# A quarter of the first expert weight by the hardware DMA queue, and a new written order for attention

## The chip, the cores and the metric

The kernel runs on one core of one Trainium2 chip. The core has a matrix engine (PE, whose weight loads are listed as PEld), a vector engine (DVE), a scalar engine (ACT), GpSimd (POOL), a sync engine (SP), and 16 DMA engines that all its queues share. The metric is the device time of one execution in microseconds (us), lower is better; of several runs the median is taken.

## What is computed

The first half is attention over 4 batches, 8 heads, 768 positions and head dimension 64. The integer input `is_retrieval` splits the heads: retrieval heads see all earlier keys, the others see the first 4 keys and the last 64.

```python
scores = scale * np.matmul(q, k.transpose(0, 1, 3, 2))
scores = np.where(mask, scores, -1000000000.0)
a = np.exp(scores - max); a = a / (sum(a) + 1e-09)
attn = np.matmul(a, v)
```

The second half is a soft mixture of 8 experts with 4 slots each over the 3072 rows x (512 wide) that attention gives:

```python
logits = x @ phi                                  # 3072 x 32
d = softmax(logits, over rows);  slot_input = d.T @ x
h = relu(slot_input[e] @ w1[e]);  slot_out[e] = h @ w2[e]      # 8 experts
out = softmax(logits, over slots) @ slot_out
```

w1 is 8 x 512 x 1024 and w2 is 8 x 1024 x 512, in float32. Inputs are 52.5 MB, the output is 6.3 MB.

## The kernel before

**Loads.** q, k and v of one batch (`load_raw`, L270) and one 512 x 1024 weight of an expert (`load_w`, L283) are each one DMA that POOL issues (L252) on the software queue; this queue turns float32 into bf16 on the way. There are 12 raw loads of 1.57 MB and 16 weight loads of 2.10 MB, as float32. They go into 11 slots of 8 KB per partition, and the last five weights (11 to 15, `late_mem`, L744) into memory that attention has left: weight 14 into `pt_mem` after PV.14.5, weight 15 into `qk_mem` after the last score matmul. Before the change nothing is loaded by SP; ACT issues two small loads (L363, L364).

**Attention.** Heads are worked in 16 pairs p = 4b + n, where b is the batch. Raw q, k, v are transposed on PE (`T` operations, L476, four per tensor and batch) and evicted from PSUM by `E` operations through the helper `copy` (L243), by DVE or by ACT. Score blocks (`QK`, L501) go into two PSUM buffers. ACT takes the exponential (`EX`, L572, five per pair, each 128 x 1024) into `pt_mem`, DVE multiplies the mask in (`MK`, L518), PE multiplies by v (`PV`, L632), DVE normalises (`NM`, L644 and L646), PE transposes the result (`XT`, L658) and a copy `XE` stores it. v needs a second transpose (`V2`, L535), a copy `VB` and a masked copy `VF` (L551). Ek1.3 is the eviction of the fourth quarter of batch 1's k, VB.7 the copy of pair 7's v, and so on.

**The tail.** After pair 15 come the logits (`LG`), their exponential (`EL`), the slot sums (`DS`, `SA`, `SI`, `SIE`), the first expert product `H` (L808) with its relu `HR`, transposes `TH`, evictions `HE`, and then the eight `W2.e` steps in order, e = 0 to 7 (L846), of eight matmuls each. W2.7 needs weight 15. Its result is scaled by ACT (`SO`, L854), multiplied out in 25 pieces (`OM`, L873; `OE`, L880 and L882) and stored by SP in 8 DMAs (L892).

**Order.** A list scheduler, class `Plan`, fixes the order of all of this when the kernel is built. Every operation has a duration per engine, dependencies, buffers to take and free, a due key (`T` = 6.2 us per pair), and for some a `lead`, the earliest start. `run` (L62) picks, among what could start within 0.12 us of the earliest, the smallest key. Where an operation names two engines (`copy_engs = {"DVE": 0.56, "ACT": 0.81}`), the scheduler picks one. `LAT` holds what it adds between an operation's end and its use on another engine. Each engine then executes its instructions strictly in the order so written.

**Fillers.** `emit_zb` (L377) starts PE with 13 matmuls on zeros. After the schedule is made, a second loop (L919 to L961) puts more zero matmuls (L965) where the plan leaves PE idle: ahead of an operation that starts by 22 us, about one for each 0.215 us of the planned gap; and in the tail, up to the start of the W2 steps.

```python
gap, at = max(o.start + shift - free, 0.0), free
unit = 0.427 if slow else 0.215
n = int((gap - 0.1) / unit + 0.5) if gap > 0.2 else 0
```

Here `o.start` is the planned time and `free` the planned end of what stands before on PE; the plan gives the 13 first matmuls 0.30 us each.

Of the kernel before, what the change touches and what calls it, by code (L numbers as in the profile page):

```python
# [10 lines left out]
F32 = mybir.dt.float32  # L11
# [4 lines left out]
ACT = mybir.ActivationFunctionType  # L16
PSUM = bass.MemoryType.PSUM
KB = 512


class Buf:


# [9 lines left out]
class Plan:  # L33


    LAT = {"PE": 0.20, "ACT": 0.06, "DVE": 0.08, "POOL": 0.15, "DMA": 0.40, "SP": 0.05}
    OVERLAP = {"ACT": 0.10, "DVE": 0.085}
    SWITCH, BONUS, ACTPEN = 0.13, 4.0, 0.4

# [4 lines left out]

    def op(self, name, engs, key, deps=(), acq=(), rel=(), emit=None, lead=0.0, need=(), n=0):
        o = Op()
        o.name, o.engs, o.key, o.emit = name, engs, key, emit
        o.deps = [d for d in deps if d is not None]
        o.acq, o.rel, o.end, o.eng, o.succ, o.lead = list(acq), list(rel), None, None, [], lead
        o.kind = ("r" if name[0] == "Q" else "c" if name[0] == "T" and name[1] in "qkv" else  # L50
                  "g" if name[:2] in ("DS", "H.", "W2") else "f")
        o.need = [b for b in list(need) + o.rel if b not in o.acq]
        for b in o.rel:
            b.rels += 1
            b.left += 1
        o.ndep, o.n = len(o.deps), n
        for d in o.deps:
            d.succ.append(o)
        self.ops.append(o)
        return o  # L60
# [88 lines left out]
def kernel(  # L149
# [13 lines left out]
    nc = tc.nc  # L163
    P = 128
    B, H, S, D = q.shape
# [13 lines left out]
    pt_mem = sb.tile([P, 20 * KB], BF16, name="pt")  # L179
# [10 lines left out]
    ident = sb.tile([P, P], BF16, name="ident")  # L190
# [12 lines left out]
    flag = sb.tile([P, 2, H], BF16, name="flag")  # L203
# [46 lines left out]
    def dma(name, key, nbytes, ndesc, buf, dst, src, deps=()):  # L250
        iss = pl.op("issue " + name, {"POOL": 0.62}, key, deps=deps, acq=[buf] if buf else [], lead=1.3,
                    emit=lambda o: nc.gpsimd.dma_start(dst(), src))  # L252
        issues.append(iss)
        return pl.op("land " + name, {"DMA": dma_us(nbytes, ndesc)}, key, deps=[iss], lead=2.8)

    def dma_us(nbytes, ndesc):
        return ndesc / 16 * 0.0225 + nbytes / 16 / 27170.0
# [12 lines left out]
    def load_raw(x, b, key):  # L270
        raws[x, b] = buf = Buf("S8")
        lands[x, b] = dma(f"{x}{b}", key, 96 * 2 * 8192, 192, buf, lambda: raw_view(buf, 0, 96), raw_src(x, b, 0, 4))
# [6 lines left out]
    def w_view(i):  # L279
        m = late_mem[i]() if i in late_mem else slots[wbuf[i].slot][:, :]  # L280
        return m.rearrange("p (a f) -> p a f", a=4 if i < NE else 8)

    def load_w(i, key, deps=()):  # L283
        if i < NE:
            src = moe_w1[i].rearrange("(di do) f -> di do f", do=4)
        else:
            src = moe_w2[i - NE].rearrange("(fi fo) d -> fi fo d", fo=8)
        wland[i] = dma(f"w{i}", key, 2 << 20, 128, None if i in late_mem else wbuf[i],
                       lambda: w_view(i), src, deps=deps)
# [72 lines left out]
    def sp_front(o):  # L362
        nc.scalar.dma_start(ri, ri_src)  # L363
        nc.scalar.dma_start(phf, moe_phi.rearrange("(di do) s -> di do s", do=4))  # L364

    load_raw("q", 0, -99)
    o_iss = pl.op("issue small", {"ACT": 1.0}, -98, emit=sp_front, lead=0.7)
    o_sp = pl.op("land small", {"SP": 0.1}, -98, deps=[o_iss], lead=3.0)
# [10 lines left out]
            nc.tensor.matmul(pvb[:, 1, :], zero[:, 0:128], zero, start=True, stop=True, skip_group_check=True)  # L379

    o_zb = pl.op("ZB", {"PE": 0.30 * NZ}, -100, n=NZ, emit=emit_zb, lead=1.2)
    o_id = pl.op("ident", {"DVE": 0.5}, -80, deps=[o_tab], emit=head_const)
    o_kp = pl.op("key_pos", {"DVE": 2.3}, -79, deps=[o_id, o_tq], emit=key_pos)
    o_fl = pl.op("flag row", {"DVE": 0.35}, -79.5, deps=[o_sp], emit=flag_row)
    o_fl = pl.op("FB", {"PE": 0.1}, -78, n=1, deps=[o_fl, o_zb], acq=[flb], emit=flag_bc)
    o_fl = pl.op("flags", {"DVE": 1.0}, -78, deps=[o_fl, o_kp], rel=[flb], emit=flags)

# [2 lines left out]
            nc.gpsimd.memset(b_[:, :, :, :, 64:66], 1.0)  # L390

    o_one = pl.op("ones", {"POOL": 0.4}, -40, deps=[issues[2]], emit=pone)
    o_fm = pl.op("far mask", {"ACT": 1.6}, -39, deps=[o_fl], emit=far_mask)
    o_hm = {}
    for n in range(4):
        o_hm[n] = [pl.op(f"hm{n}.{i}", {"DVE": 0.55}, -28.5 if n == 0 else T * n - 2.0, deps=[o_fl],
                         emit=lambda o, h=n + 4 * i: head_mask(h)) for i in range(2)]
    o_st = pl.op("slot tables", {"DVE": 1.2}, T * 8, deps=[o_id], emit=slot_tables)

    phb = xT.rearrange("p a c -> p (a c)")[:, 2048:2176].rearrange("p (o s) -> p o s", o=4)  # L400
    ph2 = xT.rearrange("p a c -> p (a c)")[0:NS, 2304:2816]
# [396 lines left out]
    for e4 in range(2):  # L798
        hse[e4] = []
        for c in range(2):  # L800
            hp = Buf("SC" if c == 0 else "TR")
            h_buf = hp if e4 == c == 0 else h_buf
            bank = (lambda hp=hp: scb[hp.slot][:, 0, :]) if c == 0 else (lambda hp=hp: trb[hp.slot])

            def emit_h(o, e4=e4, c=c, bank=bank):
                for do in range(4):
                    for g in range(4):
                        nc.tensor.matmul(bank()[32 * g:32 * (g + 1), :], siT[:, do, :],  # L808
                                         w_view(4 * e4 + g)[:, do, c * 512:(c + 1) * 512],
                                         start=(do == 0), stop=(do == 3), tile_position=(0, 32 * g))  # L810

            a = pl.op(f"H.{e4}.{c}", {"PE": 0.86}, kt + 1, n=16, deps=[o_sie] + [wland[4 * e4 + g] for g in range(4)],
                      acq=[hp], emit=emit_h)

            def emit_hr(o, e4=e4, c=c, bank=bank):
                d, s_ = hs_t[e4][:, c, :], bank()
                if o.eng == "ACT":
                    nc.scalar.activation(d, s_, ACT.Relu, scale=emask[:, e4:e4 + 1])
                else:
                    nc.vector.tensor_scalar(d, s_, emask[:, e4:e4 + 1], 0.0, op0=ALU.mult, op1=ALU.max)  # L820

            hse[e4].append(pl.op(f"HR.{e4}.{c}", {"ACT": 0.7, "DVE": 0.76}, kt + 1, deps=[a, o_st],
                                 rel=[hp], emit=emit_hr))
        th = Buf("SC")

        def emit_th(o, e4=e4, th=th):
            t = scb[th.slot][:, 0, :].bitcast(BF16)
            hv = hs_t[e4].rearrange("p c f -> p (c f)").rearrange("p (fi fo) -> p fo fi", fo=8)
            for fo in range(8):
                nc.tensor.transpose(t[:, 128 * fo:128 * (fo + 1)], hv[:, fo, :], ident)  # L830

        a = pl.op(f"TH.{e4}", {"PE": 0.5}, kt + 2, n=8, deps=hse[e4], acq=[th], emit=emit_th)

        def emit_he(o, e4=e4, th=th):
            copy(o, hT_t[e4].rearrange("p f c -> p (f c)"), scb[th.slot][:, 0, :].bitcast(BF16))

        hte[e4] = pl.op(f"HE.{e4}", {"DVE": 0.7, "ACT": 1.02}, kt + 2, deps=[a], rel=[th], emit=emit_he)
# [81 lines left out]
    for o in order:  # L919
        if o.eng != "PE":  # L920
            continue
        if o is o_zb:
            hist += [(o.start + 0.30 * (x + 1), 512) for x in range(NZ)]
            free = o.end
            continue
        gap, at = max(o.start + shift - free, 0.0), free
        tail = at >= last_pv - 0.01 and o.start <= w_last.start + 0.01
        front = o.start <= 22.0
        if front:
            start = max(o.start + shift, free)  # L930
            slow = start < 4.2
            unit = 0.427 if slow else 0.215
            n = int((gap - 0.1) / unit + 0.5) if gap > 0.2 else 0
            for _ in range(n):
                hist.append((free + unit, 512))
                free += unit
            took = (o.end - o.start) * (1.7 if slow else 1.0)
            while o.start > 4.5:
                e = max(free, o.start + shift) + took
                got = sum(a for t, a in hist if t > e - FW) + area(o.name)  # L940
                if got >= FA or n >= 6:
                    break
                n += 1
                free += unit
                hist.append((free, 512))
            free = max(free, o.start + shift) + took
            hist.append((free, area(o.name)))
            if n:
                if at < first_pv:
                    before[o.name] = (n, 0, pvb[:, 1, :], 0)  # L950
            continue
        free = o.end
        gap = o.start - at
        if gap < 0.25 or not tail or (at >= by_name["W2.0"].end - 0.01 and o is not w_last):
            continue
        if o is w_last:
            continue
        bank, c0 = (scb[h_buf.slot] if o.start <= h_first + 0.01 else pvb)[:, 1, :], 0
        us, w = gap - 0.12, 512 - c0
        n = max(0, int(us / (w / 2400)))  # L960
        before[o.name] = (n, max(0, int((us - n * w / 2400) / 0.0534)), bank, c0)  # L961

# [45 lines left out]
```

## Time and profile before

| | |
|---|---|
| median of 3 runs | 153.15 us (153.1 to 153.8) |
| the profiled execution | 152.3 us |
| its span, first to last instruction | 150.4 us |
| busy: PE, DVE, ACT, POOL | 126.7, 112.1, 109.7, 17.9 us |
| software queue (loads) | 26.22 MB written as bf16, 85.4% of the 16 engines' span |
| hardware queue (stores) | 6.29 MB, 10.3% |
| mean granted TensorE clock | 0.973 |

All durations below are of the one profiled execution. A busy PE is not a PE at its peak, and the share of a DMA engine can pass 1 where its packets overlap. The engines' busy times are means over stages that have different limits, so a stage has to be looked at by itself. A line number is that of the kernel before.

### The profile page before, as it was taken

The page shows a single profiled execution, that of the slowest core. Times are in us where ns is not written, and L with a number is a line of the kernel's source. Part 1 is how long each engine was busy: PE and PEld are TensorE (multiplying, and loading weights), DVE is VectorE, ACT ScalarE, POOL GpSimd, SP SyncE. Part 2 cuts the span into 40 slices and gives each one's busy share as a digit, 9 for nine tenths or more (in the row PEclk, how much of TensorE's full clock was granted, in tenths as well). Part 3 has the DMA queues.
Part 4 walks back from the last instruction along what each step waited for, and adds up shares of the span by engine and source line. Part 5 has one row for each costly group of instructions (what it writes and reads, how often), then busy time and mean ns, then how long its engine had stood idle before and what let it go on. Part 6 is the DMA issues. An engine that isn't in the chain of part 4 may idle for free.

```text
span 150.4 us, 5213 instructions
## 1 busy us (share of the span) xinstructions
PE 126.7 (84%) x2299; PEld 81.6 (54%) x2304; DVE 112.1 (75%) x232; ACT 109.7 (73%) x132; POOL 17.9 (12%) x37
## 2 busy tenths in 40 slices
PE   6999999988899999698999899999779999797000
PEld 2355566757667676565757667666457446332000
DVE  3879579989689979967998978979866495099000
ACT  3053899997998999689999999999993243299000
POOL 6911110101110001210000112110011000000000
PEclk9999999999999999999999999999999999999955
DMA  3999999999999999999999999999999997069993
GB/s 40 190 215 220 220 206 211 216 221 216 211 211 217 217 220 218 218 205 215 212 219 228 211 200 211 218 218 213 213 216 213 222 218 163 13 229 438 425 420 161
DMA packets 6120, 32.90 MB, mean 219 GB/s; under 512 B 594, under 2 KB 722, under 8 KB 3410
## 3 DMA queue, kind: packets, MB, share of 16 engines
q0 software_dynamic: 4800, 26.22, 85.4%
q1 hardware_dynamic: 1152, 6.29, 10.3%
q8 instruction: 18, 0.29, 0.7%
q10 hardware_dynamic: 146, 0.07, 0.2%
q14 instruction: 4, 0.03, 0.1%
HBM read 52.49 MB, written 6.29 MB: 391 GB/s over the span
## 4 chain that ended last, share of the span: by engine, by line
PE 31%; DMA 20%; issue 15%; ACT 13%; DVE 12%; POOL 2%; DVEq 0%; POOLq 0%; ACTq 0%
DMA qk<-in_moe_w_dram 11%; ACT pt L572 9%; DMA slot<-in_v_dram 9%; PE tr L476 8%; PE pv L632 8%; PE sc L501 8%; DVE slot L882 3%; DVE pt L518 2%; DVE xv L646 2%; PE tr L658 2%; DVE vf L551 1%; ACT xv L245 1%; ACT vx L596 1%; DVE vx L247 1%; PE tr L673 1%
## 5 line engine op out<-in xcount | busy, mean ns | idle before, releaser
L572 ACT ACTIVATE pt<-sc 128x1024 bf16<-128x1024 f32 x80 | 77.0, 1054 | 4.3 <-PE sc L501 4.1
L501 PE MATMUL sc<-qk 64*128 64x512 bf16 (+3 forms) x256 | 31.0, 307 | 4.4 <-ACT pt L572 2.7
L518 DVE TENSOR_TENSOR pt<-pt,msk 128x1024 bf16<-128x1024 bf16 (+1 forms) x48 | 30.6, 640 | 1.8 <-ACT pt L572 1.6
L632 PE MATMUL pv<-vx,pt 128*128 128x65 bf16 x352 | 27.2, 193 | 0.3 <-DVE pt L518 0.2
L632 PEld LDWEIGHTS <-pt 128*128 128x128 bf16 x640 | 23.6, 97 | 6.9 <-issue 4.1
L476 PE MATMUL tr<-ident,slot 96*64 96x96 bf16 x704 | 20.8, 208 | 2.2 <-issue 1.8
L476 PEld LDWEIGHTS <-slot 96*64 96x64 bf16 x768 | 18.3, 110 | 8.0 <-issue 5.9
L632 PE MATMUL pv<-vf,pt 128*128 128x65 bf16 x288 | 21.4, 194 | 0.0
L501 PEld LDWEIGHTS <-qk 64*128 64x128 bf16 x256 | 11.0, 93 | 12.6 <-issue 6.3
L646 DVE TENSOR_TENSOR xv<-pv,rs 128x768 bf16<-128x768 f32 x16 | 15.3, 958 | 0.6
L247 DVE COPY qk<-tr 128x768 bf16<-128x768 bf16 x22 | 11.8, 551 | 1.5 <-PE tr L476 1.3
L252 POOL DMA_DIRECT2D slot<-in_moe_w_dram x11 | 6.0, 550 | 41.1 <-PE tr L476 31.7
L247 DVE COPY xT<-tr 128x768 bf16<-128x768 bf16 x15 | 8.3, 553 | 1.1 <-PE tr L658 1.1
L658 PE MATMUL tr<-ident,xv 128*128 128x128 bf16 x96 | 8.0, 220 | 1.1 <-DVE xv L646 0.9
L247 DVE COPY xv<-tr 128x768 bf16<-128x768 bf16 x10 | 5.5, 555 | 3.7 <-PE tr L476 3.5
L245 ACT COPY qk<-tr 128x768 bf16<-128x768 bf16 x6 | 4.8, 816 | 4.3 <-PE tr L476 4.2
L658 PEld LDWEIGHTS <-xv 128*128 128x128 bf16 x96 | 5.8, 97 | 3.9 <-issue 1.8
L535 PE MATMUL tr<-ident,xv 128*128 128x128 bf16 x96 | 7.8, 220 | 0.1
L965 PE MATMUL pv<-zero 128*128 128x512 bf16 (+1 forms) x31 | 7.4, 365 | 0.5 <-issue 0.5
L551 DVE TENSOR_TENSOR vf<-vx,fm 128x528 bf16<-128x528 bf16 x16 | 6.7, 429 | 1.2 <-ACT vx L245 1.0
L644 DVE RECIPROCAL rs<-pv 128x12 f32<-128x12 f32 x16 | 3.7, 230 | 5.1 <-PE pv L632 4.8
L535 PEld LDWEIGHTS <-xv 128*128 128x128 bf16 x96 | 5.6, 97 | 2.2 <-issue 1.4
(114 smaller groups left out, 155.1 us busy)
## 6 DMA issues: line engine op xcount, KB each, us to landing
slot<-in_moe_w_dram POOLq DMA_DIRECT2D x11, 1024.0 KB, 23.8
out_dram<-slot SPq DMA_DIRECT2D x5, 1024.0 KB, 6.6
slot<-in_q_dram POOLq DMA_DIRECT2D x4, 768.0 KB, 27.1
slot<-in_k_dram POOLq DMA_DIRECT2D x4, 768.0 KB, 28.2
slot<-in_v_dram POOLq DMA_DIRECT2D x4, 768.0 KB, 23.5
qk<-in_moe_w_dram POOLq DMA_DIRECT2D x2, 1024.0 KB, 15.3
vx<-in_moe_w_dram POOLq DMA_DIRECT2D x1, 1024.0 KB, 20.7
xv<-in_moe_w_dram POOLq DMA_DIRECT2D x1, 1024.0 KB, 19.1
```

The source lines that it names most:

```text
L245: nc.scalar.copy(dst, src)
L247: nc.vector.tensor_copy(dst, src)
L476: nc.tensor.transpose(t[64 * i:64 * (i + 1), :, s, :], rv[:, i, 8 * c + s, :], ident[0:96, 0:96])
L501: nc.tensor.matmul(scb[sc.slot][:, i, c:c + 128 * nb], kk, qq.rearrange("p b c -> p (b c)"), start=True, stop=True)
L518: nc.vector.tensor_tensor(pw, pw, mw, op=ALU.mult)
L535: nc.tensor.transpose(t[:, 128 * j:128 * (j + 1)], vT[:, 6 * n + j, :], ident)
L551: nc.vector.tensor_tensor(vfs[VFb[p].slot], vv, fm[:, n], op=ALU.mult)
L572: nc.scalar.activation(pTs[PTb[b, n].slot][:, :, 512 * g:512 * (g + 1)], scb[sc.slot], ACT.Exp, scale=scale)
L632: nc.tensor.matmul(pvb[:, h, 65 * i:65 * (i + 1)], lt, rhs, start=(j == 0), stop=(j == i))
L646: nc.vector.tensor_tensor(xo, pvw[:, :, :, 0:64], r.rearrange("p i (j o) -> p i j o", o=1).to_broadcast([P, 2, 6, 64]), op=ALU.mult)
L658: nc.tensor.transpose(t[:, 128 * i:128 * (i + 1)], xv[:, i, 128 * n:128 * (n + 1)], ident)
L965: nc.tensor.matmul(bank[:, c0:c0 + w], zero[:, 0:128], zero[:, 0:w], start=(c0 == 0), stop=True, skip_group_check=True)
```

## The change

The change has four parts.

1. Weight 0 is loaded in two pieces. One quarter of its rows (of each four, the first: 0.52 MB of float32) is loaded by SP on the hardware queue as the first DMA of the program, into `wf`, a float32 view of the first 4 KB of each partition's `pt_mem`. ACT then casts it into its place in the slot (`CW`, 128 x 1024). The software queue loads the other three quarters. The first `H` step waits for `CW` too.
2. 76 operations get their due key moved by up to 8 us (`SHIFT`), and 15 copies get a fixed engine (`ALT`: the number is the place in the operation's list of engines; for `E` and `VB` operations 0 is DVE and 1 is ACT).
3. Constants of the scheduler change: 1.30 instead of 0.40 after a DMA, 1.0 for the new "HW" resource, `lead` 3.3 instead of 2.8 for a software load, and the durations of five operations of the front.
4. Fillers are also put between the W2 steps and ahead of W2.7; ahead of a W2 step 1.0 us of the planned gap is left free instead of 0.12.

```diff
+SHIFT = {
+    "Tq1.0": -3.5, "Tk1.2": 6, "Tk2.0": 5.5, "Tv2.0": -0.5, "Tv2.1": 5, "Tv2.3": -7.5, "Tk3.1": 6.5, "Ek3.2": 3.5,
...
+    "QK.1.0": -8, "QK.1.4": 4, "VF.2": -2, "QK.2.2": 2.5, "QK.2.3": -4, "QK.2.4": 3, "MK.2.2": -3.5, "VF.3": -7,
...
+    "TE.1": 8, "PV.8.3": 8, "PV.10.0": 2.5, "PV.11.3": -3.5, "TE.2": 5, "PV.12.4": 8, "XE.12": 8, "XT.14": 8,
+}
+ALT = {
+    "Eq0.0": 1, "Eq0.2": 1, "Eq0.3": 1, "Ek0.1": 0, "Ek1.1": 0, "Ek1.3": 0, "Ev1.0": 0, "Ek2.1": 0, "Eq3.0": 0,
+    "Ev3.0": 0, "Ev3.3": 1, "VB.0": 1, "VB.4": 1, "VB.7": 1, "VB.11": 1,
+}
-    LAT = {"PE": 0.20, "ACT": 0.06, "DVE": 0.08, "POOL": 0.15, "DMA": 0.40, "SP": 0.05}
+    LAT = {"PE": 0.20, "ACT": 0.06, "DVE": 0.08, "POOL": 0.15, "HW": 1.0, "DMA": 1.30, "SP": 0.05}
-        o.name, o.engs, o.key, o.emit = name, engs, key, emit
+        if name in ALT:
+            engs = dict([list(engs.items())[ALT[name]]])
+        o.name, o.engs, o.key, o.emit = name, engs, key + SHIFT.get(name, 0.0), emit
-        return pl.op("land " + name, {"DMA": dma_us(nbytes, ndesc)}, key, deps=[iss], lead=2.8)
+        return pl.op("land " + name, {"DMA": dma_us(nbytes, ndesc)}, key, deps=[iss], lead=3.3)
     def load_w(i, key, deps=()):
+        if i == 0:
+            src = moe_w1[0].rearrange("(di do) f -> di do f", do=4)[:, 1:4, :]
+            wland[i] = dma("w0", key, 3 << 19, 128, wbuf[0], lambda: w_view(0)[:, 1:4, :], src)
+            cast = pl.op("CW", {"ACT": 1.1}, -90, deps=[wland_first], need=[wbuf[0]],
+                         emit=lambda o: nc.scalar.copy(w_view(0)[:, 0, :], wf))
+            w_cast.append(cast)
+            return
+    wf = pt_mem[:, 0:4 * KB].bitcast(F32)
+    w_cast = []
+    o_wf = pl.op("issue wf", {"SP": 0.45}, -99, lead=0.7, emit=lambda o: nc.sync.dma_start(
+        wf, moe_w1[0].rearrange("(di do) f -> di do f", do=4)[:, 0, :]))
+    wland_first = pl.op("land wf", {"HW": 1.2}, -99, deps=[o_wf], lead=1.75)
-    o_id = pl.op("ident", {"DVE": 0.5}, -80, deps=[o_tab], emit=head_const)
-    o_kp = pl.op("key_pos", {"DVE": 2.3}, -79, deps=[o_id, o_tq], emit=key_pos)
-    o_fl = pl.op("flag row", {"DVE": 0.35}, -79.5, deps=[o_sp], emit=flag_row)
+    o_id = pl.op("ident", {"DVE": 0.75}, -80, deps=[o_tab], emit=head_const)
+    o_kp = pl.op("key_pos", {"DVE": 2.45}, -79, deps=[o_id, o_tq], emit=key_pos)
+    o_fl = pl.op("flag row", {"DVE": 0.5}, -79.5, deps=[o_sp], emit=flag_row)
...
-    o_fm = pl.op("far mask", {"ACT": 1.6}, -39, deps=[o_fl], emit=far_mask)
+    o_fm = pl.op("far mask", {"ACT": 2.2}, -39, deps=[o_fl], emit=far_mask)
...
-            a = pl.op(f"H.{e4}.{c}", {"PE": 0.86}, kt + 1, n=16, deps=[o_sie] + [wland[4 * e4 + g] for g in range(4)],
+            a = pl.op(f"H.{e4}.{c}", {"PE": 0.86}, kt + 1, n=16, deps=[o_sie] + [wland[4 * e4 + g] for g in range(4)] + (w_cast if e4 == 0 else []),
...
-        if gap < 0.25 or not tail or (at >= by_name["W2.0"].end - 0.01 and o is not w_last):
-            continue
-        if o is w_last:
+        if gap < 0.25 or not tail:
             continue
         bank, c0 = (scb[h_buf.slot] if o.start <= h_first + 0.01 else pvb)[:, 1, :], 0
-        us, w = gap - 0.12, 512 - c0
+        us, w = gap - (1.0 if o.name[:2] == "W2" else 0.12), 512 - c0
```

## The prediction

> **What bounds the kernel now.** I read the page's head first, then DMA share by stretch, then the order of time at both ends of attention, then ACT's waits.
>
> ```profile
> span 150.4 us, 5213 instructions
> PE 126.7 (84%) x2299; PEld 81.6 (54%) x2304; DVE 112.1 (75%) x232; ACT 109.7 (73%) x132; POOL 17.9 (12%) x37
> DMA  3999999999999999999999999999999997069993
> q0 software_dynamic: 4800, 26.22, 85.4%
> q1 hardware_dynamic: 1152, 6.29, 10.3%
> ```
>
> The DMA row is full from the second slice to the 33rd: the loads never pause, so taking bytes out of them ends them earlier. The hole in slice 35 lies between the last load and the first store. Stretches tell where loading begins and ends (start and end, length, the engines' busy times, clock, DMA share, GB/s):
>
> ```profile
> 0.00:2.00 2.00, 0.81 (x2) 0.28 (x3) 0.27 (x1) 0.32 (x1) 0.90 (x5) 1.00 0.00 0
> 2.80:3.20 0.40, 0.40 (x2) 0.15 (x1) 0.40 (x2) 0.17 (x1) 0.39 (x2) 1.00 0.94 72
> 128.80:129.50 0.70, 0.70 (x16) 0.31 (x9) 0.00 (x0) 0.00 (x0) 0.00 (x0) 1.00 0.06 12
> 133.00:148.50 15.50, 4.99 (x17) 1.43 (x15) 6.35 (x10) 5.87 (x11) 0.00 (x0) 0.80 1.00 406
> 15.58:114.20 98.62, 90.21 (x1875) 63.96 (x1875) 83.70 (x159) 92.69 (x104) 10.17 (x18) 1.00 1.04 215
> ```
>
> No DMA moves before 2.0 us; loading fills 2.8 to 129.5, some 126.7 us. Now the tail, from the order of time, and the chain at its last load:
>
> ```profile
> 128.60 0.60 PE L846 MATMUL pv<-xv,xT 128*32 128x512 bf16 x8
> 129.03 0.60 PE L846 MATMUL pv<-pt,xT 128*32 128x512 bf16 x8
> 129.76 0.62 PE L846 MATMUL pv<-qk,xT 128*32 128x512 bf16 x8
> ...
> 113.38 16.34 DMA qk<-in_moe_w_dram
> ```
>
> These are W2.5, W2.6 and W2.7. W2.7 starts when weight 15 lands (113.38 + 16.34 = 129.72). But W2 steps start 0.43 us apart (129.03 - 128.60), so PE by itself would have started W2.7 at 129.03 + 0.43 = 129.46. **Two paths end within 0.3 us of each other:** path A, the loads; path B, attention and the expert chain behind it. A gain on A alone is worth 0.3 us. Everything behind W2.7 (SO, the OM pieces, 15.5 us of stores) moves with it.
>
> Path B is attention's end plus a fixed chain, so what bounds attention matters. Exponentials run from 15.58 to 114.20, and in these 98.62 us ACT is busy 92.69: ACT bounds, with 5.9 us of idle time. Its largest wait:
>
> ```profile
> ACT pt L572 <- PE sc L501: 4.1, 9, 1.4
> ```
>
> Nine times ACT waits for score matmuls, longest 1.4 us: PE runs in written order and was late with them. The front, again in order of time:
>
> ```profile
> 1.19 5.27 PE L379 MATMUL pv<-zero 128*128 128x512 bf16 x13 [1.19 <-DVE zero L374]
> 6.50 1.90 PE L965 MATMUL pv<-zero 128*128 128x512 bf16 x8
> 8.52 0.53 PE L476 MATMUL sc<-ident,slot 96*64 96x96 bf16 x16
> 12.48 0.53 PE L476 MATMUL sc<-ident,slot 96*64 96x96 bf16 x16
> 15.58 1.94 ACT L572 ACTIVATE pt<-sc 128x1024 bf16<-128x1024 f32 x2 [0.69 <-PE sc L501]
> 16.80 0.87 PE L476 MATMUL tr<-ident,slot 96*64 96x96 bf16 x32
> ```
>
> Zero matmuls until 8.40, q's first transposes at 8.52 when q lands, k's at 12.48, the first exponential at 15.58, v's transposes at 16.80.
>
> **The change, part by part.** *The quarter on the hardware queue.* It takes 0.52 of 52.4 MB from the software loads, 1.0% of 126.7 us: 1.27 us. On the hardware queue the stores move 6.29 MB in 15.5 us, so 0.52 MB takes 1.29 us. It is the program's first DMA, and no engine works before 2.0 us. ACT's first small load, at 0.73, moved its bytes some 0.9 us after its issue; the same delay on SP, issued near 0.7, gives 1.6 to 2.9, 0.1 us into q's load. If SP is late by a quarter of the load or more, the overlap is up to 0.5 us and q loses that. So path A gains 0.8 to 1.27 us; I take 1.0, the middle: weight 15 lands near 128.7. SP has nothing else until its stores at 132; POOL issues as many DMAs as before, in the same order.
>
> Here the Trainium skill speaks against the change: its page "DMA: Bandwidth & Descriptors", section "Issuing engines are not separate DMA queues", says that DMAs of SP, ACT and POOL run on the same 16 engines and interleave, and that another issuer saves only issue time. By that rule alone the gain is nil, and it is a rival below.
>
> *CW*: one ACT copy of 128 x 1024 from float32. The exponentials of that size take 0.97 us (1.94 for two). ACT is free from 2.96 (its table load) to 7.94, the load lands near 4, so CW ends by 5.2: nothing. Uncovered, above 3 us later, it would push the far mask, for which VF first needs at 21.10.
>
> *Engines of 15 copies.* In order of time the trace shows which copies ran where. Of the 15, Ek1.3 (36.48), Ev1.0 (37.17) and Ev3.0 (89.32) ran on ACT among the exponentials and go to DVE; VB.0 (20.50) and VB.7 (60.49) ran on DVE and go to ACT; VB.4, VB.11 and Ev3.3 were on ACT already, Ek1.1, Ek2.1 and Eq3.0, as far as the order tells, on DVE; Eq0.0, 0.2 and 0.3 go to ACT before the first exponential, where it idles. Net one copy less on ACT: 0.7 us (copies at 36.48 and 37.17 start 0.69 apart). DVE is busy 83.70 of 98.62 us and can carry one more of 0.55. The 30 or so copies not fixed can move too; if two more changed side, that is 1.4 us either way.
>
> *The new order.* It can win at most ACT's idle 5.9 us, and lose as much again if new waits are as many. Nearest row: the 4.1 us of nine waits on score matmuls. The shifts pull score matmuls of pairs 1, 8, 9, 12 and 13 ahead by 7 to 8 us, and these are what ACT waits for; I take a quarter to half of that row back, 1.0 to 2.0, say 1.5.
>
> *Fillers in front, the part that speaks against.* Their number follows from the code. Before, q is planned to land at 2.8 + 3.89, plus 0.40: its transposes at 7.09. The 13 zeros are planned to end at 5.1, the flag broadcast at 5.33. A gap of 1.76 us gives 8 fillers, as the trace has. After, the plan has 3.3 + 3.89 + 1.30 = 8.49, and a gap of 3.16 gives 14. But the 13 zeros really end at 6.46, not 5.1. So 14 fillers, at 1.90 / 8 = 0.24 us, or at the full rate's 0.21, run from 6.50 to 9.5 to 9.8, and q's transposes start up to 1.3 us after 8.52. Behind them stand four transposes and the same 11 fillers as now, then k's transposes: 13.6 instead of 12.48. The first exponential becomes some 0.85 us later, as the evictions of k, no longer queued behind q's on DVE, win back about 0.3; v's transposes go from 16.80 to 17.5. ACT is the bound from there, but its idle time absorbs some: 0 to 1.3, I take 0.8.
>
> *Path B*: -0.7 - 1.5 + 0.8 = -1.4 us, so PE alone could start W2.7 at 128.1.
>
> *Fillers before W2.7.* The plan's own landing of weight 15 is 3.3 + 125.5 of loading + 1.30 = 130.1, later than my 128.7. Zeros fill the planned gap less 1.0 us, so they can hold PE until about 129.1 if PE is on plan. Between 0 and 0.5, I take 0.2. The granted clock is 1.00 through the OM pieces already, so they win nothing.
>
> *Sum.* W2.7 at 128.7 + 0.2 = 128.9 instead of 129.76: 0.9 us. The profiled execution took 152.3 (span 150.4 and 1.9 around it), 0.85 under the median of 153.15. So 151.4 on its own scale, and 152.2 against the median.
>
> **The rivals.** *Path B stands*: savings and the filler delay cancel within 0.6 us. For it: two paths 0.3 us apart; an order fitted to planned times, where the plan misses the 13 zeros by 1.4 us. Against: three copies leave ACT. W2.7 at 129.0 to 130.0, middle 129.5: 0.3 us less, 152.9.
>
> *The quarter saves no engine time* (the page's rule): the same 16 engines pay 1.29 us for it before q moves on, so q, k, v and all weights keep their times. For it: DMA share is already 0.94 at 2.8, where the queue starts. Against: it is 0.00 until 2.0. W2.7 at 129.7: 153.1.
>
> *The fillers hold up the front* (slower): 6 more zeros delay q's and k's transposes by the full 1.3 us, ACT never idles where it counts, and the new order wins only what one copy less gives. For it: the trace's 8 and 11 fillers agree with the code's arithmetic, and q's transposes start right behind the 8 today. Against: PE has waits behind. Decides from 1.1 us of net delay on path B (129.46 to 130.5). With the delay at 1.3, the moved copies worth nothing (their exchange undone by the free ones), and one more wait of the longest size, 1.4, as the new order's price in front, where score matmuls of pair 0 change places behind these zeros: 129.46 + 2.7 = 132.2 at worst, 130.8 without that wait. Middle 131.0: 1.25 us more, 154.4.
>
> **How the numbers follow.** Forecast 0.43; path B stands 0.25; no engine time saved 0.06; fillers hold up the front 0.26. About 0.5% (0.77 us) is what can be told from no change; 152.4 and 153.9 are the bounds. The forecast is all faster: 0.43; the two middle cases are within: 0.31; the last is slower: 0.26. Forecast alone: from 151.9 (A's whole 1.27, no filler cost) to 152.4 (A at 0.8; with more filler cost than that it counts as the second case). The range: runs lie 0.3 us and more around a median (153.1 to 153.8), so 151.3 below; above, the slower case to a little past its middle, 154.6, which leaves out about 0.1 on that side and less below.
>
> **What would show it.** Right: DMA share over zero by 2.0 us; weight 15 landing near 128.7; CW over by 6 us; 14 fillers before q's first transpose, which starts near 9.7; three named copies on DVE, two on ACT; ACT's waits for score matmuls under 3 us; W2.6 started by 128.3, and W2.7 at the landing or right behind a filler. Wrong: exponentials that end after 114.2, which puts path B in front; q landing later than 9.0, which means the quarter was paid for; or an idle ACT in the middle of attention behind a moved PV or transpose.

## The result and the profile after

The changed kernel takes 154.37 us (median of 17 runs, 153.39 to 157.87); the kernel before, run beside it, 152.22 us (17 runs, 151.95 to 153.8). The ratio is 1.0115, 95% interval [1.009, 1.014]: slower by about 1.75 us, where 0.9 us faster was forecast. The profiled execution after took 153.97 us with a span of 152.1; the one before, 152.3 with 150.4. The spans differ by 1.7 us. A few executions fall in a slower state (157.86 and 157.87 us here), which the ratios, and the medians of the experiments below, leave out; of the profiled executions that of experiment 4 is in it.

First the head of the page after, the DMA row of its slices and its queues (packets, MB, share):

```profile
span 152.1 us, 5257 instructions
DMA  5999999999999999999999999999999994059994
q0 software_dynamic: 4800, 25.95, 83.7%
q1 hardware_dynamic: 1296, 6.82, 11.5%
```

The quarter is there: the hardware queue has 144 packets and 0.53 MB more, and the first slice shows 5 instead of 3. But the loads still end in slice 34. Now PE's order of time in the tail (start, length, engine, line and operation; in brackets what ended an idle time ahead):

```profile
125.03 0.60 PE L880 MATMUL pv<-xv,xT 128*32 128x512 bf16 x8
125.79 1.57 PE L997 MATMUL pv<-zero 128*128 128x512 bf16 x8 [0.16 <-issue]
127.29 0.62 PE L880 MATMUL pv<-pt,xT 128*32 128x512 bf16 x8
127.84 3.74 PE L997 MATMUL pv<-zero 128*128 128x512 bf16 x18
131.51 0.61 PE L880 MATMUL pv<-qk,xT 128*32 128x512 bf16 x8
```

W2.5, W2.6 and W2.7 are the first, third and fifth line. The two between are new: 8 zeros ahead of W2.6, 18 ahead of W2.7, with no idle time behind them. The issues of weights 14 and 15 on POOL, and their rows among the DMA issues (KB, us from issue to landing):

```profile
109.00 0.53 POOL L273 DMA_DIRECT2D pt<-in_moe_w_dram  x1 [8.44 <-PE pv L666]
109.52 0.54 POOL L273 DMA_DIRECT2D qk<-in_moe_w_dram  x1
```

```profile
pt<-in_moe_w_dram POOLq DMA_DIRECT2D x1, 1024.0 KB, 15.7
qk<-in_moe_w_dram POOLq DMA_DIRECT2D x1, 1024.0 KB, 20.1
```

Weight 15: 109.52 + 20.1 = 129.6, to the hundredth 129.66; before it was 129.72. W2.7 could have started there and started at 131.51. **The 1.85 us of zeros behind the landing are the whole loss**: W2.7 is 131.51 - 129.76 = 1.75 us later than before, and what stands behind it takes as long as before (152.1 - 131.51 = 20.6 us, 150.4 - 129.76 = 20.6 us). It takes both fillings to make it. Weight 14 had landed at 124.7 (109.00 + 15.7), so W2.6 could have followed W2.5 by 0.43 us, at 125.46; behind the 8 zeros it came 1.83 us later. Without these 8 the 18 would have ended near 129.7, at the landing of weight 15. That is an estimate from these rows, as no run kept the 18 alone.

Two more things are in this view. W2.5 starts at 125.03 instead of 128.60, so attention and the expert chain became 3.57 us faster, and none of it reaches the end. And weight 15 lands when it landed before, so the quarter brought nothing. The front shows why the second is so:

```profile
6.46 3.19 PE L997 MATMUL pv<-zero 128*128 128x512 bf16 x14
10.07 0.53 PE L510 MATMUL sc<-ident,slot 96*64 96x96 bf16 x16 [0.42 <-DMA slot<-in_q_dram]
16.83 3.88 ACT L606 ACTIVATE pt<-sc 128x1024 bf16<-128x1024 f32 x4 [0.74 <-PE sc L535]
```

```profile
1.31 8.72 DMA slot<-in_q_dram
```

The second fence is a line of the chain: q's load, issued at 1.31, lands at 10.03; before, q's transposes started with it at 8.52. All 14 zeros are there, and they did not hold up q: they were over at 9.65 and PE waited 0.42 us more for q itself.

Two stretches of the front (start and end, length, busy times of the engines, clock, DMA share, GB/s), and the whole of the exponentials:

```profile
1.00:2.00 1.00, 0.82 (x2) 0.28 (x3) 0.13 (x1) 0.31 (x1) 0.69 (x1) 1.00 0.19 37
2.00:3.00 1.00, 1.00 (x4) 0.44 (x3) 0.42 (x2) 0.97 (x1) 0.91 (x4) 1.00 0.94 254
...
16.83:110.44 93.61, 87.92 (x1852) 62.43 (x1850) 83.52 (x159) 90.90 (x101) 10.17 (x18) 1.00 1.04 214
```

```profile
ACT pt L606 <- PE sc L535: 2.4, 8, 0.7
```

The quarter's bytes move from 1.75 us on, as forecast. They then take until 4.81, 3.06 us for 0.52 MB, and the software queue's first packet comes at 3.61 instead of 2.78. Attention: 93.61 us from first to last exponential instead of 98.62, with ACT idle for 2.7 instead of 5.9 us and busy for 90.90 instead of 92.69. Its wait for score matmuls fell from 4.1 us (longest 1.4) to 2.4 (longest 0.7).

### The profile page after: what moved, and what is told of

The parts are those of the page before. It is cut to its first block, busy times and chain, and to the rows that moved or that the text cites. A ratio compares the mean times of both kernels' runs of the same rounds, so it can differ in the third digit from the quotient of the medians.

```text
span 152.1 us, 5257 instructions
## 1 busy us (share of the span) xinstructions
PE 130.8 (86%) x2328; PEld 83.3 (55%) x2333; DVE 111.5 (73%) x232; ACT 111.2 (73%) x133; POOL 17.8 (12%) x37
## 4 chain that ended last, share of the span: by engine, by line
PE 52%; ACT 24%; DMA 6%; issue 5%; DVE 5%; DVEq 0%; ACTq 0%; POOLq 0%
ACT pt L606 22%; PE sc L535 10%; PE pv L666 10%; PE tr L510 7%; PE pv L997 7%; DMA slot<-in_q_dram 6%; DVE slot L916 3%; PE pv L880 3%; PE tr L569 2%; PE tr L692 2%; PE tr L707 1%; PE sc L997 1%; PE sc L842 1%; PE tr L842 1%; PE sc L510 1%
## 5 line engine op out<-in xcount | busy, mean ns | idle before, releaser
L666 PE MATMUL pv<-vx,pt 128*128 128x65 bf16 x352 | 26.3, 193 | 0.1
L510 PE MATMUL tr<-ident,slot 96*64 96x96 bf16 x704 | 22.0, 208 | 0.7 <-issue 0.7
L535 PEld LDWEIGHTS <-qk 64*128 64x128 bf16 x256 | 10.1, 94 | 14.3 <-issue 9.2
L997 PE MATMUL pv<-zero 128*128 128x512 bf16 (+1 forms) x62 | 13.6, 362 | 0.5 <-issue 0.5
L997 PEld LDWEIGHTS <-zero 128*128 128x128 bf16 x82 | 7.0, 97 | 7.9 <-issue 1.3
L916 DVE TENSOR_SCALAR slot<-tr,rrow 128x512 f32<-128x512 f32 (+1 forms) x5 | 3.3, 692 | 9.6 <-PE tr L907 9.6
L268 DVE COPY xv<-tr 128x768 bf16<-128x768 bf16 x14 | 7.5, 552 | 3.9 <-PE tr L510 3.8
L268 DVE COPY xT<-tr 128x768 bf16<-128x768 bf16 x13 | 7.2, 555 | 1.7 <-PE tr L692 1.6
L888 ACT ACTIVATE msk<-pv,rcs 128x512 bf16<-128x512 f32 x1 | 0.7, 687 | 10.0 <-PE pv L880 10.0
L569 PEld LDWEIGHTS <-xv 128*128 128x128 bf16 x96 | 5.7, 97 | 2.0 <-issue 1.3
```

Source lines behind the costliest of these rows:

```text
L268: nc.vector.tensor_copy(dst, src)
L510: nc.tensor.transpose(t[64 * i:64 * (i + 1), :, s, :], rv[:, i, 8 * c + s, :], ident[0:96, 0:96])
L535: nc.tensor.matmul(scb[sc.slot][:, i, c:c + 128 * nb], kk, qq.rearrange("p b c -> p (b c)"), start=True, stop=True)
L569: nc.tensor.transpose(t[:, 128 * j:128 * (j + 1)], vT[:, 6 * n + j, :], ident)
L666: nc.tensor.matmul(pvb[:, h, 65 * i:65 * (i + 1)], lt, rhs, start=(j == 0), stop=(j == i))
L916: nc.vector.tensor_scalar(d, bank(), sc_, None, op0=ALU.mult)
```

## Experiments

Ratios are to the kernel before, run on the same chip. All kernels compute the whole result. "The zeros" are the filler matmuls that the filler function puts ahead of named steps.

**1. No zeros ahead of W2 steps.** If the zeros made the loss, it goes with them.

```diff
-        if gap < 0.25 or not tail:
+        if gap < 0.25 or not tail or o.name[:2] == "W2":
```

> The changed kernel without any zero matmuls among the W2 steps; all else of the change stays. Theory Z (the zeros ahead of W2.6 and W2.7 make the loss): W2.6 ends near 126.0, PE then stands idle until weight 15 lands at 129.7, W2.7 starts at 129.7 instead of 131.5, so the span falls by 1.8 us, to 150.3, and the ratio to the kernel before is 0.997 to 1.004. If the idle 3.7 us costs TensorE its clock, the 25 output pieces start at half rate and up to 0.6 us of this is given back. Theory O (the new order or the late front makes the loss): the ratio stays at 1.010 to 1.014.

153.41 us against 152.16, ratio 1.0065 [1.0033, 1.0097]. Span 151.5.

```profile
126.72 0.60 PE L880 MATMUL pv<-pt,xT 128*32 128x512 bf16 x8
130.74 0.62 PE L880 MATMUL pv<-qk,xT 128*32 128x512 bf16 x8 [3.41 <-DMA qk<-in_moe_w_dram]
...
133.03 0.63 PE L907 MATMUL pv<-msk,expT 128*128 128x512 bf16 x1
```

```profile
PEclk9999999999999999999999999999999999959855
```

W2.7 now starts 0.04 us behind the landing (130.70), so nothing but the load holds it. In place of the zeros PE idles for 3.41 us, and the clock row drops to 5 one slice later: 0.50 from 132.53 to 135.94, where an output matmul takes 0.63 instead of 0.38 us. The stores behind hide nearly all of it in this execution: from W2.7 to the end of the span it is 20.8 us here and 20.6 us in the kernel before. Weight 15 lands 1.0 us later here than in the changed kernel; the next runs show how far that moves by itself. The ratio of 1.0065 lies between the two expectations: a part of the loss went with the zeros. In the profiled execution, whose span is 1.1 us above the kernel before, what is left is the later landing, 1.0 us, and the slower clock, about 0.1.

**2. Fourteen zeros.** So many fit between W2.6 and the landing; ahead of W2.6 there are none.

```diff
+        if o is w_last:
+            before[o.name] = (14, 0, pvb[:, 1, :], 0)
-        if gap < 0.25 or not tail:
+        if gap < 0.25 or not tail or o.name[:2] == "W2":
             continue
```

> As the run without zeros among the W2 steps, but with 14 zero matmuls ahead of W2.7 alone, which at 0.213 us each end 3.0 us after W2.6, at 129.1, before weight 15 lands. Theory Z: W2.7 at 129.7, the clock stays at 1.00, span 150.3, ratio 0.996 to 1.003. Theory O: 1.010 to 1.014. Against the run with none, this one tells what the clock costs: equal if the clock holds without zeros, 0.3 to 0.6 us faster if it does not.

152.69 us against 152.16, ratio 1.0018 [0.9987, 1.0049].

```profile
126.11 3.19 PE L999 MATMUL pv<-zero 128*128 128x512 bf16 x14
130.26 0.61 PE L880 MATMUL pv<-qk,xT 128*32 128x512 bf16 x8 [0.95 <-DMA qk<-in_moe_w_dram]
...
132.30 0.38 PE L907 MATMUL pv<-msk,expT 128*128 128x512 bf16 x1
```

The zeros end 0.95 us ahead of the landing, the clock holds (0.38 us a matmul) and the loss is gone: from 1.0115 to 1.0018. The zeros were 1.0% of the time, about 1.5 us. Against experiment 1 the two profiled executions differ by 0.7 us (153.37 and 152.69), of which 0.5 are the earlier landing and about 0.1 the clock. The intervals overlap, but in 111 of the 132 pairs of one execution of each (12 and 11) the one with 14 zeros is the faster. Its mean granted clocks are all 0.967 to 0.976, and those of experiment 1 are 0.946 to 0.954 in nine of the twelve, its profiled one having 0.960. So the 14 zeros are likely better than none, and the clock costs most executions more than the 0.1 us of this pair; how much is not shown. With the same loads, weight 15 landed at 129.66, 130.70 and 130.22 in the three executions. This scatter of a microsecond in one profile is as wide as the quarter's forecast gain, so a gain has to be told from the times of several executions.

**3. The change without its quarter.** Experiment 2, weight 0 whole by the software queue, no CW; the written order is otherwise that of the change.

```diff
+        if o.name in ("issue wf", "CW"):
+            continue
+        if o.name == "issue w0":
+            nc.gpsimd.dma_start(w_view(0), moe_w1[0].rearrange("(di do) f -> di do f", do=4))
+            continue
```

> The order, engines and 14 zeros of the run before this, but weight 0 whole on the software queue, with no load by SP and no cast; the written order is held. Theory Q (the quarter saves nothing, since q pays for it): q lands at 8.5 instead of 10.0, weight 15 still lands at 129.5 to 129.9, and the time equals that of the run with the quarter within 0.3 us. Rival S (the quarter saves its 1.27 us and something else of the change eats it): weight 15 lands at 130.5 to 131, and the time is 0.8 to 1.3 us above the run with the quarter.

152.42 us against 152.16, ratio 1.0015 [0.9989, 1.0042].

```profile
9.58 0.53 PE L510 MATMUL sc<-ident,slot 96*64 96x96 bf16 x16
...
16.34 1.94 ACT L606 ACTIVATE pt<-sc 128x1024 bf16<-128x1024 f32 x2 [0.74 <-PE sc L535]
...
122.56 0.61 PE L880 MATMUL pv<-slot,xT 128*32 128x512 bf16 x8
...
125.70 3.20 PE L999 MATMUL pv<-zero 128*128 128x512 bf16 x14
129.70 0.61 PE L880 MATMUL pv<-qk,xT 128*32 128x512 bf16 x8 [0.80 <-DMA qk<-in_moe_w_dram]
```

1.0015 without the quarter, 1.0018 with it: **no gain of the quarter is to be seen**. The two intervals leave room for a few tenths of a microsecond, but not for the forecast 0.8 and more. The new order and engines, by themselves, take as long as the kernel before, though W2.0 starts at 122.56 instead of 126.43: their 3.9 us lie in the shadow of weight 15. Without the quarter q lands at 8.63, but its transposes start at 9.58: here the 14 zeros do hold them up.

**4. The quarter alone**, in the kernel before, with its own order and its 8 and 11 zeros in front.

```diff
+    wf = pt_mem[:, 0:4 * KB].bitcast(F32)
+    src0 = moe_w1[0].rearrange("(di do) f -> di do f", do=4)
+    nc.sync.dma_start(wf, src0[:, 0, :])
...
+        if o.name == "issue w0":
+            nc.gpsimd.dma_start(w_view(0)[:, 1:4, :], src0[:, 1:4, :])
+            nc.scalar.copy(w_view(0)[:, 0, :], wf)
+            continue
```

> The kernel before with the first part of the change alone: the quarter by SP, the cast on ACT, its own order and fillers held. Theory Q: q lands near 10.0 instead of 8.5, weight 15 lands at 129.5 to 129.8 as before; as path B has only 0.3 us to spare here and its front starts up to 1.5 us later, W2.7 comes 0.2 to 1.3 us later, ratio 1.001 to 1.009. Rival S: weight 15 lands at 128.5, ratio 0.993 to 1.000.

153.78 us against 152.16, ratio 1.0096 [1.0054, 1.0138]: slower, the quarter alone does harm. The profiled execution took 155.8 us, 2.0 above that median, so what it shows is one way of losing time; that the median's 1.0% comes about in the same way is not shown.

```profile
11.00 0.53 PE L476 MATMUL sc<-ident,slot 96*64 96x96 bf16 x16 [2.80 <-DMA slot<-in_q_dram]
...
12.60 4.06 PE L965 MATMUL pv<-zero 128*128 128x512 bf16 x11
```

```profile
PEclk9995999999999999999999999999999999999855
```

q lands at 10.96, the 8 zeros are over at 8.2, PE idles for 2.80 us, and the clock drops to 0.5 from 12.29 to 15.70, while the next 11 zeros run (4.06 us instead of 2.32). The first exponential starts at 19.74 and W2.0 at 130.35, 4.2 and 3.9 us later than before: the old order passes the delay on. Weight 15 lands at 131.68, and W2.7 follows W2.6 by 0.43 us at 133.38, so here path B ends last. The 6 extra zeros in front, which the prediction counted as a price, may be what keeps the clock up until the later q in the changed kernel; that kernel was not run without them. How much of the 1.0% this is was not measured by itself.

**5. Half of weight 0 by the hardware queue.** Rows of 8 KB instead of 4 KB, two casts; else experiment 2.

```diff
+        if o.name == "issue wf":
+            nc.sync.dma_start(pt_mem[:, 0:8 * KB].bitcast(F32).rearrange("p (a f) -> p a f", a=2),
+                              moe_w1[0].rearrange("(di do) f -> di do f", do=4)[:, 0:2, :])
+            continue
+        if o.name == "issue w0":
+            nc.gpsimd.dma_start(w_view(0)[:, 2:4, :], moe_w1[0].rearrange("(di do) f -> di do f", do=4)[:, 2:4, :])
+            continue
...
```

> The kernel with 14 zeros ahead of W2.7, and half of weight 0 (1.05 MB, rows of 8 KB instead of 4 KB per partition) by SP with two casts. Theory Q1 (the quarter gains nothing because the software queue's start slides behind it, whatever its size): q lands later than 10.0, near 11.5, weight 15 at 129.6 to 130.3, ratio 0.998 to 1.006. Theory Q2 (the quarter was too slow in itself, 0.52 MB in 3.1 us, because its rows are short, and it ends before the software queue runs at full rate): the half moves at twice the rate, covers that start, by 20 us at least 0.3 MB more has been moved than before, weight 15 lands at 128.5 to 129.2 and the ratio is 0.992 to 0.997.

152.2 us against 152.25, ratio 0.9988 [0.9957, 1.0019].

```profile
3.00:4.00 1.00, 1.00 (x4) 0.33 (x3) 0.88 (x8) 0.00 (x0) 0.99 (x3) 1.00 0.90 377
...
127.00:128.00 1.00, 1.00 (x6) 0.47 (x5) 0.00 (x0) 0.00 (x0) 0.00 (x0) 1.00 0.18 41
128.00:129.00 1.00, 0.87 (x5) 0.29 (x3) 0.00 (x0) 0.00 (x0) 0.00 (x0) 1.00 0.05 8
```

```profile
129.27 0.61 PE L880 MATMUL pv<-qk,xT 128*32 128x512 bf16 x8 [0.40 <-DMA qk<-in_moe_w_dram]
```

1.05 MB took 3.74 us (1.74 to 5.48), 280 GB/s, against 171 for the quarter, and W2.7 starts at 129.27. q lands at 10.02, no later than with the quarter. Counted in bytes of float32 read since the start, this kernel is 0.45 MB ahead of the kernel before at 20 us and 0.26 MB at 120 us, and that of experiment 10, which has the same half, 0.44 and 0.22 MB. The three executions with the quarter (the changed kernel, experiments 1 and 2) are from 0.08 MB ahead to 0.09 behind at 20 us, and from 0.04 ahead to 0.29 behind at 120 us. So bytes can be won with the half, though the times do not yet tell it from no change. The last two stretches show where part of it goes: from 127 us on the DMA share is 0.18, about 3 of 16 engines by an estimate from that share, and the load goes on for two more microseconds.

**6. The quarter by itself.** Experiment 2 with five repeated iotas (fills of an index table, 0.69 us each) first on POOL, so that the software loads begin only when the quarter is over.

```diff
+        if o.name == "issue q0":
+            for _ in range(5):
+                tables_q(o)
```

> The kernel with 14 zeros and the quarter, with five more iotas on POOL (0.69 us each) ahead of its first load, so that q's load is issued near 4.8 instead of 1.31 and the quarter runs by itself. Theory C (the quarter took 3.1 us because it shared the engines with q's load): by itself it moves in 1.3 to 1.8 us from 1.75, over by 3.5, and lands by 4.0. Theory H (short rows on the hardware queue are slow in themselves): it is over at 4.2 to 4.8 again. Both: everything behind it is 3 to 3.5 us late, the time 2.5 to 3.5 us above the kernel with 14 zeros.

One execution, 154.47 us, as the loads start later: 1.8 us above the 152.69 of experiment 2, less than expected. The stretches in which nothing but ACT's two small loads (0.07 MB) runs beside the quarter:

```profile
2.00:3.00 1.00, 1.00 (x4) 0.43 (x3) 0.00 (x0) 0.96 (x1) 0.89 (x2) 1.00 0.95 270
3.00:4.00 1.00, 1.00 (x4) 0.32 (x3) 0.00 (x0) 0.00 (x0) 0.91 (x2) 1.00 0.68 250
4.00:5.00 1.00, 1.00 (x5) 0.37 (x4) 0.00 (x0) 0.20 (x1) 1.00 (x2) 1.00 0.13 40
```

1.76 to 4.43, so 2.67 us and 196 GB/s; 3.06 us in the changed kernel. The price of 1.29 us, taken from the stores, was too low in itself, and sharing the engines with q's load adds only 0.4 us. The software queue's first packet comes 1.5 us after its issue here (4.36 to 5.86), and 2.3 us after it in the changed kernel (1.31 to 3.61).

**7. Fewer zeros in front.** Experiment 3, with the plan's end of the 13 zeros put 1.23 us later, which leaves 9 zeros instead of 14.

```diff
-            free = o.end
+            free = o.end + 1.23
```

> The run without the quarter, with the planned end of the 13 first zeros set 1.23 us later, to what the trace has: 9 zeros instead of 14 ahead of q's transposes. If the 5 extra zeros were the price of the front: q's transposes start at 8.6 instead of 9.58, the first exponential at 15.4 to 15.7 instead of 16.34, and W2.0 comes up to 0.8 us before 122.56. If ACT's idle time later absorbs it, W2.0 stays at 122.3 to 122.8. Either way weight 15 sets the end and the time stays within 0.3 us.

One execution, 153.52 us.

```profile
8.64 0.53 PE L510 MATMUL sc<-ident,slot 96*64 96x96 bf16 x16 [0.90 <-DMA slot<-in_q_dram]
...
15.40 1.02 ACT L606 ACTIVATE pt<-sc 128x1024 bf16<-128x1024 f32 x1 [0.74 <-PE sc L535]
...
122.89 1.48 PE L880 MATMUL pv<-slot,xT 128*32 128x512 bf16 x24
```

q's transposes and the first exponential start 0.94 us earlier than in experiment 3, and W2.0 at 122.89 instead of 122.56. That attention absorbs a delay at its start does not rest on this pair alone: in seven executions with the new order (the changed kernel, experiments 2, 3, 5, 7, 8 and 10) the first exponential starts between 15.40 and 17.48 us, and W2.0 stays within 122.48 and 122.98; only in experiments 1 and 6, which start at 17.50 and 18.28, does it come at 124.12 and 124.28. The time is 1.1 us above experiment 3, not within the 0.3 expected, because weight 15 landed at 130.87. Its last 8 KB packet ended at 129.41; the 4-byte packet that closes the queue ended at 129.83, right behind a 16 KB packet of the instruction queue (128.86 to 129.82), and the landing came 1.0 us later still, where it was 0.3 to 0.5 us in the other executions. No run was made on the cause of that.

**8. Weight 15 in two loads**, 120 and 8 partitions, in the hope that the engines that end last then have less of it. Else experiment 3.

```diff
+        if o.name == "issue w15":
+            for r in (slice(0, 120), slice(120, 128)):
+                nc.gpsimd.dma_start(w_view(15)[r], moe_w2[7].rearrange("(fi fo) d -> fi fo d", fo=8)[r])
+            continue
```

> The run without the quarter, with weight 15 in two software loads, of 120 and of 8 partitions. In the last 3 us of loading the share of busy DMA engines falls from 1.05 to 0.06, so some engines end up to 3 us after the others. If the two pieces spread differently over the engines and the late ones get less, weight 15 lands 0.5 to 1.5 us before 129.65 and the ratio is 0.990 to 0.997; if they get as much or more, it lands at 129.6 to 130.5 and the ratio is 1.000 to 1.007.

152.61 us against 152.25, ratio 1.0004 [0.9978, 1.003]. The two loads landed at 130.11 and 130.26 (20.5 and 20.1 us after their issues): no gain.

**9. The engines without the keys.** Experiment 1 with the 15 fixed engines and the new constants, but with SHIFT left out.

```diff
-        o.name, o.engs, o.key, o.emit = name, engs, key + SHIFT.get(name, 0.0), emit
+        o.name, o.engs, o.key, o.emit = name, engs, key, emit
```

> The kernel without zeros among the W2 steps, with the 15 fixed engines and the new constants, but no key moved. Theory P (the plan's differences hold on the chip): its plan puts W2.0 at 127.0 where the whole change has 119.7, and the chip ran the whole change 3.1 us behind its plan, so W2.0 comes at 129.8 to 130.6, W2.7 at 132.8 to 133.7 and the time is 3 to 4 us above the kernel before. Rival (the fixed engines carry the gain of path B, one copy less on ACT being worth 0.7 us or more, and the keys are noise): W2.0 at 122.9 to 126.0.

One execution, 154.41 us.

```profile
128.81 1.48 PE L880 MATMUL pv<-slot,xT 128*32 128x512 bf16 x24
...
132.04 0.61 PE L880 MATMUL pv<-qk,xT 128*32 128x512 bf16 x8
```

W2.0 starts at 128.81: 2.4 us later than before, 4.7 us later than experiment 1. That is short of the 129.8 expected from the plan, and far from the rival's 126.0 at most. The code's own arithmetic, run without the chip, points the same way: it plans W2.0 at 119.72 with both, at 127.01 with the engines alone, at 126.04 with the keys alone and at 124.96 with neither. By the plan, each half of the search's answer is worse than nothing without the other; the chip has shown this for the engines alone, in one execution, where 127.01 - 119.72 = 7.3 us were planned, and 4.7 measured against experiment 1 or 5.95 against the changed kernel (122.86). The keys alone were not run.

**10. The best of it, and SO split.** Experiment 5, with SO's first half on ACT and its second on DVE.

```diff
-        nc.scalar.activation(slot_out, pvb[:, 0, :], ACT.Copy, scale=rcs[:, 0:1])
+        nc.scalar.activation(slot_out[:, 0:256], pvb[:, 0, 0:256], ACT.Copy, scale=rcs[:, 0:1])
+        nc.vector.tensor_scalar(slot_out[:, 256:512], pvb[:, 0, 256:512], rcs[:, 0:1], None, op0=ALU.mult)
```

> The kernel with half of weight 0 by SP, with the scaling behind W2.7 (SO, 0.69 us on ACT) split in two halves of 256 columns, ACT and DVE side by side. The first output piece needs ACT's half alone: it starts 0.2 to 0.3 us earlier after W2.7, and so do the stores. Weight 15 at 128.9 to 129.6. Ratio 0.993 to 0.999: below the kernel before by what the half gave (0.1%) and 0.15% more. If DVE's half is the later one, the second piece waits and the gain is under 0.1 us.

151.89 us against 152.29, ratio 0.9968 [0.9942, 0.9995]: faster than both kernels, by a little.

```profile
128.79 0.61 PE L880 MATMUL pv<-qk,xT 128*32 128x512 bf16 x8
...
129.45 0.47 ACT L888 ACTIVATE msk<-pv,rcs 128x256 bf16<-128x256 f32 x1 [7.66 <-PE pv L880]
129.96 0.48 DVE L889 TENSOR_SCALAR msk<-pv,rcs 128x256 bf16<-128x256 f32 x1 [6.60 <-ACT msk L888]
```

The split isn't the reason: DVE's half waited for ACT's, and the first store came 3.42 us after W2.7, against 3.23 in experiment 5. W2.7 itself is earlier, 128.79. That the half on 8 KB rows is what wins is likely, with 128.74 and 129.22 as the earliest landings of all kernels here, but two kernels' intervals, one of which holds 1, don't prove it.

## Why the prediction was wrong

**Fillers before W2.7: the step that failed.** "Between 0 and 0.5, I take 0.2" measured 1.85 us. The bound held only if PE was on plan, as the step itself said, and PE was not. The plan has W2.0 at 119.72; the chip started it at 122.86, 3.1 us behind. The plan's W2.6 ends at 125.55 and its W2.7 starts at 130.12; the gap of 4.57 less 1.0 was filled to the end. On the chip W2.6 ran at 127.29, and the same filling stood 2.3 us later. The signs of it were in the prediction's own text: it had found the plan 1.4 us off at the 13 zeros (6.46 against 5.1; the plan itself ends them at 5.23, so 1.23). In the trace of before, too, W2.0 was 2.4 us behind its planned time (126.43, planned 124.04). Applied here, that lag alone puts the end of the zeros at 130.12 - 1.0 + 2.4 = 131.5, 1.8 us past the landing. The step also missed the 8 zeros ahead of W2.6. They come from the same edit of the condition and lie on the same path: the plan has W2.6 wait for weight 14 until 125.11, while on the chip weight 14 had landed at 124.7 and W2.6, 1.83 us later for the zeros, had nothing to wait for.

**The quarter, "0.8 to 1.27":** measured 0.06 us in the profile, 1.0018 against 1.0015 in time. Two prices were wrong. The stores' rate (406 GB/s) was taken for rows of 4 KB at the program's start, where 171 to 196 were measured. And the software queue was taken to start when it did before; it started 0.83 us later. q landed at 10.03, which the prediction had named as the sign that "the quarter was paid for". The rival with the chance of 0.06, that no engine time is saved, is what happened to path A. The Trainium skill's rule ("DMA: Bandwidth & Descriptors", section "Issuing engines are not separate DMA queues") gave that result, and the runs agree with it for the quarter. They go beyond it for the half: what moves before the software queue starts is time that no other load used, and at 280 GB/s 0.22 to 0.26 MB of it were still won at 120 us.

**Path B, "-1.4":** measured 3.57 us, the right sign with well under half of the size. In the profiles ACT's idle time fell by 3.2 us (the order, for which 1.5 was taken) and its busy time by 1.8 us (three copies fewer among the exponentials, not one: 13 instead of 16); the first exponential came 1.25 us later. The step "fillers in front", 0.8, was no cost to path B at all, as experiment 7 shows. What the prediction had right is the frame: two paths 0.3 us apart, so that a gain on one is worth 0.3 us. By it, once path A stands, 3.57 us on path B cannot show, and experiment 3 measured just that.

**The slower rival** gave 154.4 us, and 154.37 was measured, but this is luck. Its scale rests on the median of three runs, 153.15, where 17 runs have 152.22; its own loss was 1.25 us and 1.75 was measured. And it put the loss in the front, which cost nothing at the end. The zeros were the right suspects in the wrong place.

**Right:** the quarter's bytes moving before 2.0 us; CW (5.18 to 6.22) for nothing, though 0.22 us past the sign named for it; 14 zeros ahead of q's transposes; the named copies on their engines (Ek1.3, Ev1.0 and Ev3.0 on DVE, VB.0 and VB.7 on ACT); ACT's waits for scores under 3 us.

## What to carry to other kernels

Filler work ahead of a step on the end's path must be sized by what the trace leaves room for, not by a plan: compare the plan's times with the trace's at the nearest step, carry the lag into the filling, and leave a margin of that size. Before pricing a gain, ask on which of two nearly equal paths it lies; here 3.6 us won on one of them were worth nothing. And a transfer's price comes from a row of the same queue with the same length of rows, with the start of the neighbouring queue priced beside it.

## What the runs showed of the hardware

- On the hardware queue, 128 rows of 4 KB took 2.67 us beside nothing but two small loads (196 GB/s) and rows of 8 KB, twice the bytes, 3.74 us (280 GB/s). An earlier load of this kind delayed the software queue's first packet by 0.83 us (3.61 against 2.78); without it, in experiment 3, that packet came at 2.80.
- PE idle for 3.41 us ahead of W2.7 was followed by a clock of 0.50 for 3.4 us (experiment 1), and idle for 2.80 us in the front by the same (experiment 4). The length of one idle time does not decide alone: ahead of W2.7, 1.41 us in experiment 6 were followed by such a drop (134.21 to 137.62) and 1.69 us in experiment 7 were not. The Trainium skill, "TensorE: Matmul & The Clock Gate", section "Part 1: The HAM clock gate (the "warmup" mystery)", gives an idle window of about 3.4 us. The first case agrees; the second, at 2.80, is shorter, but 1.29 us of transposes stand between it and the drop, 4.09 us in all, and no run here tells whether they count as idle.
- The last load's end is ragged: between 127 and 128 us the DMA share is 0.51 in the kernel before and 0.18 in experiment 5, and the landing comes at 129.72 and 129.22. Fewer partitions for the last piece didn't help (1.0004).
